# Linear attention into a SwiGLU block: reordering the first batches' attention, and group 0's layer 2, on one core

## The chip, the cores and the metric

The kernel runs on one core of a Trainium2 chip. A core has TensorE (PE, matrix multiplication, results into PSUM), VectorE (DVE), ScalarE (ACT), GpSimd (POOL) and SyncE (SP), each with its own queue of instructions, and 16 DMA engines. The metric is the device time of one execution in microseconds; lower is better.

## What is computed

```python
# q, k, v: 8 batches x 8 heads x 576 positions x 64;  phi(x) = elu(x) + 1
q_p, k_p = phi(q), phi(k)
kv  = einsum('bhsd,bhse->bhde', k_p, v)
z   = sum(k_p, axis=2)
num = einsum('bhsd,bhde->bhse', q_p, kv)
den = einsum('bhsd,bhd->bhs', q_p, z)[..., None] + 1e-06
x   = (num / den).transpose(0, 2, 1, 3).reshape(4608, 512)
g   = x @ w_gate                       # 512 x 1536
out = (g * sigmoid(g)) * (x @ w_val) @ w_out     # 1536 x 512
```

The kernel computes phi as max(x, 0) + min(exp(x), 1).

## The kernel before

Every batch of 576 positions is cut in 9 units of 64 (`J = 9`); 8 units make a group of 512 rows, so there are 9 groups for 8 batches (`NG = 9`), and group 1 holds the last unit of batch 0 and most of batch 1. For each group, layer 1 runs over 12 blocks of 128 hidden features (`fb`). Each block takes 8 matmuls of 128x512, four chunks of the 512 inputs for the gate and four for the value (`l1`, L285, or chunk by chunk with `l1_mm`, L270). ACT then takes silu of the gate half, and DVE multiplies it with the value half into `hT` (`l1_post`, L278). Layer 2 runs over four row tiles `t`, 12 matmuls each (`l2_mm`, L295), which `l2_out` (L311) moves from PSUM to `osb` and stores.

The attention of later batches is worked in between. For a batch, `exp_k`, `mx_k`, `mn_k` and `add_k` make phi(k) in `kp`; `kv_corner` (L176) makes k.v from it in 36 matmuls of 64x64 for each half of the heads (`lp`), with either `kp` alone, or the terms `kp` (holding the max) and `ek` (holding the min) one after the other; `r_copy` moves it to `R`. The sum over positions z is made in two ways. In batches 2 to 7, `zsum` on DVE and `zb` (L207) on PE and ACT spread it over the partitions; then `chain` (L506) makes den on DVE, for half of the heads at a time: `s3_prod`, `s3_reduce`, `s3_recip`, `s3_scale`, after which `dtr` (L229) transposes the scaled q by a DMA on SP's queue. In batches 0 and 1, which come before there is anything to hide behind, q is transposed on PE (`qtr`, L363), z is spread in `Zr`, den comes from PE by `t_corners(…, Zr, …)` (L411), `lnrd` (L399) makes 1/den on ACT as exp(-ln), and `x_t` (L407) multiplies num by it on DVE straight into the layer's input `xT`. `num` (L255) and `corners` (L247) make num in PSUM; `x_copy` (L261) copies it to `xT`.

PSUM is eight tiles of 128x512, used as four pairs; `ring` is the order in which `pair()` hands them out. `put_off` moves a pair to the end. The program text gives the order on every engine (the schedule is by hand), and waits between engines come from the tiles that are read and written.

At the start (L420 to L471) batch 0's attention is worked alone, then layer 1's first two blocks chunk by chunk. `warm(n)` (L120) issues `n` matmuls of 128x128 ones on PE whose result is not used; `WARM` (L43) holds how many at five places. Group 0's layer 2 is `layer2_0` (L527): all four tiles go along together, one `fb` at a time, and at given `fb` the steps `s0` to `s7` work on batch 1: transposes (`s0`, `s1`, `s3`), den (`s2`, `s4`), k.v (`s5`, `s6`), num (`s6`, `s7`), and in `s7` the last two units of batch 1 (`corners(…, 7, 9, …)`), which belong to group 2. The four evictions and the products of those last two units come at the end (`s8`). The main loop starts at L608; `block` (L516) works the attention of the next group ahead of tile 3. The line `gate` (L640) is a copy on GpSimd that reads the last transposed column, so that the loads after it in GpSimd's queue wait for it.

Of the kernel before, what the change touches and what calls it, by code (L numbers as in the profile page):

```python
# [13 lines left out]
P = 128  # L14
# [3 lines left out]
def kernel(  # L18
# [21 lines left out]
    EPS = 1e-6  # L40
    SC = 4096.0
    NB = 3
    WARM = (36, 10, 20, 8, 6)  # L43

    sb = ctx.enter_context(tc.tile_pool(name="sb", bufs=1))
    pp = ctx.enter_context(tc.tile_pool(name="ps", bufs=1, space=bass.MemoryType.PSUM))
# [50 lines left out]
    def put_off(p):  # L97
        pair(p)
# [18 lines left out]
    def act(out, in_, func=AF.Copy, scale=1.0, bias=0.0):  # L117
        nc.scalar.activation(out=out, in_=in_, func=func, bias=bias, scale=scale)  # L118

    def warm(n):  # L120
        for _ in range(n):
            nc.tensor.matmul(out=pp4[2][1][:, 0:P], lhsT=ones[:, :], rhs=ones[:, :], start=True, stop=True)

    def hs(lp):
        return slice(2 * lp, 2 * lp + 2)
# [13 lines left out]
    def mx_k(b, lp):  # L139
        nc.vector.tensor_scalar(out=jl(kp, b, lp), in0=lj(kr, b, lp), scalar1=0.0, scalar2=None, op0=ALU.max)  # L140
# [13 lines left out]
    def add_k(b, lp):  # L154
        a = kp[b % 2][:, lp, :, :]
        nc.vector.tensor_tensor(out=a, in0=ek[b % 2][:, lp, :, :], in1=a, op=ALU.add)  # L156
# [19 lines left out]
    def kv_corner(b, lp, t, first, last):  # L176
        ps = kvp[b]
        for j in range(J):
            for l2 in range(2):
                for hh in range(2):  # L180
                    rows = slice(C * hh, C * hh + C)
                    nc.tensor.matmul(out=ps[hh][D * l2:D * l2 + D, D * lp:D * lp + D],  # L182
                                     lhsT=t[b % 2][rows, lp, j, D * l2:D * l2 + D],
                                     rhs=vr[b % NB][rows, 2 * lp + l2, D * j:D * j + D],
                                     start=(first and j == 0), stop=(last and j == J - 1))
# [204 lines left out]
    def zt(b, lp, ps, t, first, last):  # L390
        for j in range(J):
            nc.tensor.matmul(out=ps[:, 0:2], lhsT=t[b % 2][:, lp, j, :], rhs=ob[:, 0:P:C],
                             start=(first and j == 0), stop=(last and j == J - 1))
# [17 lines left out]
    def t_corners(g, W, lp, ps):  # L411
        for (b, j0, j1, c0) in units(g)[1]:
            corners(ps, W[b], b, lp, j0, j1, c0)

    def t_add_half(lp, ps, h):
        a = qT[0][:, lp, 4 * h:4 * h + 4, :, :].rearrange("p j h c -> p (j h c)")
        nc.vector.scalar_tensor_tensor(out=a, in0=ps[:, 256 * h:256 * h + 256].bitcast(FP16), scalar=0.0, in1=a,
                                       op0=ALU.max, op1=ALU.add)
# [14 lines left out]
    ph[0][2]()  # L433
    mx_k(0, 0)
    zt(0, 0, pp4[3][0], kp, True, False)
    warm(WARM[3])
    mn_k(0, 0)
    zt(0, 0, pp4[3][0], ek, False, True)
    ph[1][1]()
    zr_copy(0, 0, pp4[3][0])  # L440
    warm(WARM[4])
    t_corners(0, Zr, 0, pp4[2])
    lnrd(pp4[2], 0)
    mx_k(0, 1)
    mn_k(0, 1)
    zt(0, 1, pp4[3][1], kp, True, False)
    zt(0, 1, pp4[3][1], ek, False, True)
    add_k(0, 0)
    kv_corner(0, 0, kp, True, True)
    zr_copy(0, 1, pp4[3][1])  # L450
    t_add_half(1, pq[1], 0)
    r_copy(0, 0, 1, "VV")
    t_add_half(1, pq[1], 1)
    t_corners(0, R, 0, pp4[0])
    x_t(0, 0, pp4[0], (0,))
    t_corners(0, Zr, 1, pp4[3])
    lnrd(pp4[3], 1)
    kv_corner(0, 1, kp, True, False)
    kv_corner(0, 1, ek, False, True)
    x_t(0, 0, pp4[0], (1,))  # L460
# [55 lines left out]
    def block(g):  # L516
        b1, b2 = g + 1, g + 2
        if b1 < NG:
            for lp in range(2):
                num(b1, lp)  # L520
                x_copy(b1, lp, "AV", 2 * C if b1 == 2 else 0)
        if b2 < B:
            kv_all(b2)
            r_copy(b2, 0, 2, "AA")
        put_off(l2p[(g, "p", 1)])

    def layer2_0():  # L527
        for t in range(4):
            l2_open(0, t)
        p1_z()  # L530
        p1_open()
        cq, dz = b1p["q"], b1p["z"]
        p8 = [t_phi_8(b, dz[0]) for b in range(2)]
        pm = [t_phi_main(1, lp, cq[lp]) for lp in range(2)]
        nc.scalar.preload_act_table_set("natural_log_exp_and_others")

        def den(lp, ps):
            t_corners(1, Zr, lp, ps)
            lnrd(ps, lp)

        def kvr(lp):
            kv_corner(1, lp, kp, True, True)
            r_copy(1, lp, lp + 1, "VV")

        def nx(lp, ps):
            t_corners(1, R, lp, ps)
            x_t(1, lp, ps)

        def s0():
            qtr(1, 0, cq[0])  # L550
            for f in pm[0]:
                f()

        def s1():
            qtr8(dz[0])
            for f in (0, 1, 2):
                for b in range(2):
                    p8[b][f]()

        def s2():  # L560
            den(0, dz)

        def s3():
            qtr(1, 1, cq[1])
            for f in pm[1]:
                f()

        def s4():
            den(1, cq)

        def s5():
            kvr(0)

        def s6():
            kvr(1)
            nx(0, cq)

        def s7():
            nx(1, dz)
            for lp in range(2):  # L580
                corners(cq, Zr[1], 1, lp, 7, 9, P * lp)
                corners(cq, R[1], 1, lp, 7, 9, 256 + P * lp)
            exp_k(2, 0)
            exp_k(2, 1)
            lnrd(cq, 0, 0, 256)

        def s8():
            for t in range(4):
                l2_out(0, t, "V")
            for l2 in range(2):  # L590
                xmul(xT[0][:, l2::2, 0:P], cq[l2][:, 256:512].rearrange("p (l c) -> p l c", l=2),
                     rd[0][:, l2, 0:256].rearrange("p (l c) -> p l c", l=2))

        step = {1: [s0], 3: [s1, s3], 6: [s2], 7: [s4], 9: [s5], 10: [s6], 11: [s7]}
        for fb in range(FB):
            if fb in step:
                for f in step[fb]:
                    f()
            for t in range(4):
                l2_mm(0, t, fb)  # L600
        s8()
        exp_q(2, 0)
        exp_q(2, 1)
        phi_k(2, 0)
        phi_k(2, 1)
        ring[:] = [dz, l2p[(0, "p", 0)], l2p[(0, "p", 1)], cq]

    for g in range(NG):  # L608
        b1, b2 = g + 1, g + 2
        if g == 0:  # L610
            sl = period0()
        else:
            sl, _ = none()
            if g == 1:
                sl[1] = [lam(zsum, b1)]
                sl[4] = [lam(phi_q, b1, 0), lam(zb, b1)]
                sl[5] = [lam(phi_q, b1, 1)]
                ch = chain(b1, 6)
            elif b1 < B:
                sl[0] = [lam(phi_q, b1, 0)]  # L620
                sl[1] = [lam(phi_q, b1, 1)]
                ch = chain(b1, 2)
            else:
                ch = {}
            for f, v_ in ch.items():
                sl[min(f, FB - 1)] += v_
        for fb in range(FB):
            if g == 0:
                if fb < 2:
                    continue  # L630
                if fb == 4:
                    ld2(k, kr, 2)
                    ld2(q, qr, 2)
                    ld2(v, vr, 2)
            l1(g, fb)
            for f in sl[fb]:
                f()
        if g + 3 < B:
            if g > 0:
                nc.gpsimd.tensor_copy(out=gate[:, :], in_=qT[b1 % 2][:, 1, J - 1, 1, C - 1:C])  # L640
            ld2(k, kr, g + 3)
            ld2(v, vr, g + 3)
            if g > 0:
                ld2(q, qr, g + 3)
        if g == 0:
            layer2_0()
            ld2(q, qr, 3)
        else:
            for t in range(4):
                if t == 0 and b2 < B:  # L650
                    exp_k(b2, 0)
                    exp_k(b2, 1)
                    exp_q(b2, 0)
                    exp_q(b2, 1)
                    phi_k(b2, 0)
                    phi_k(b2, 1)
                    zsum(b2)
                if g == 1 and t == 2:
                    kv_all(b1)
                    r_copy(b1, 0, 2, "AA")  # L660
                if t == 3:
                    block(g)
                if g == NG - 1 and t == 3:
                    l2_open(g, t)
                    o = None
                    for (n0, n1) in ((0, 256), (256, 512)):
                        for fb in range(FB):
                            l2_mm(g, t, fb, n0, n1)
                        o = l2_out(g, t, "V" if n0 == 0 else "A", n0, n1, o)
                    continue  # L670
                lay2(g, t)
                l2_out(g, t, "AV"[t % 2])
            if b2 < B:
                zb(b2)

# [29 lines left out]
```

## Time and profile before

| | us |
|---|---|
| median of 6 runs | 319.46 |
| the six runs | 319.17, 320.62, 319.76, 319.12, 320.64, 319.03 |
| the profiled execution | 319.38 |
| its span, first to last instruction | 317.5 |
| PE busy | 309.0 |
| DVE busy | 203.7 |
| ACT busy | 150.8 |
| POOL busy | 48.8 |

What lies around the span in the profiled execution is 319.38 - 317.5 = 1.9 us. In the views below, a line of the chain or the timeline begins with its start and its length in us, from the span's start. "x4" is four instructions merged in one line. The bracket at a line's end is the idle time of that engine before it and what ended it. PEld is the weight load, which overlaps matmuls.

### The profile page before, as it was taken

How to read it: one execution, taken by the hardware profiler on the slowest of the kernel's cores; microseconds unless marked ns; L12 is line 12 of the kernel's file. 1: busy time of each engine (PE TensorE's matmuls, PEld its weight loads, DVE VectorE, ACT ScalarE, POOL GpSimd, SP SyncE). 2: the span in 40 equal slices, each digit the busy share in tenths (PEclk: the TensorE clock that was granted, in tenths of full speed). 3: DMA queues.
4: the chain of work that ended last, by engine and by line, in shares of the span. 5: the costliest groups of instructions: out<-in, count | busy, mean ns of one | idle time of the engine just before them, and what ended most of it. 6: DMA issues, size and time to landing. Idle time of an engine off the chain costs nothing.

```text
span 317.5 us, 5702 instructions
## 1 busy us (share of the span) xinstructions
PE 309.0 (97%) x2276; PEld 146.9 (46%) x2276; DVE 203.7 (64%) x356; ACT 150.8 (47%) x227; POOL 48.8 (15%) x73
## 2 busy tenths in 40 slices
PE   7899999999999999999999999999999999999994
PEld 6634444444544454445444454445444444444443
DVE  3844866999759774987498749973992344234410
ACT  2865859737443574347534753375331333133311
POOL 8665333000500140005000600000000000000000
PEclk9989999999999999999999999999999999999999
DMA  8999999921793299038903790315023400140014
GB/s 157 195 198 199 206 206 206 254 46 37 124 234 59 56 125 233 2 74 124 236 1 74 113 241 6 61 28 121 0 42 67 99 3 1 33 101 0 0 33 101
DMA packets 41163, 32.52 MB, mean 102 GB/s; under 512 B 16432, under 2 KB 36400, under 8 KB 41136
## 3 DMA queue, kind: packets, MB, share of 16 engines
q0 software_dynamic: 20736, 18.58, 38.0%
q1 hardware_dynamic: 20320, 13.51, 17.5%
q8 instruction: 18, 0.29, 0.4%
q10 hardware_dynamic: 80, 0.07, 0.1%
q14 instruction: 9, 0.07, 0.1%
HBM read 37.75 MB, written 9.44 MB: 149 GB/s over the span
## 4 chain that ended last, share of the span: by engine, by line
PE 87%; ACT 5%; DVE 4%; DMA 2%; issue 1%; POOLq 0%
PE pp L289 54%; PE pp L296 27%; DMA qr<-in_q_dram 2%; PE pp L251 2%; PE pp L182 2%; PE pp L273 2%; DVE hT L282 1%; ACT lnt L118 1%; ACT ek L118 1%; ACT rd L118 1%; ACT eq L118 1%; PE pp L367 1%; ACT L118 0%; DVE den L217 0%; ACT sil L118 0%
## 5 line engine op out<-in xcount | busy, mean ns | idle before, releaser
L118 ACT ACTIVATE sil<-pp 128x512 f16<-128x512 f32 x108 | 63.3, 597 | 102.5 <-PE pp L289 96.1
L289 PE MATMUL pp<-xT,wg 128*128 128x512 f16 x424 | 108.8, 379 | 0.0
L289 PE MATMUL pp<-xT,wv 128*128 128x512 f16 x424 | 108.8, 379 | 0.0
L282 DVE SCALAR_TENSOR_TENSOR hT<-pp,sil 128x512 f16<-128x512 f32 x108 | 72.1, 681 | 47.8 <-PE pp L289 34.5
L296 PE MATMUL pp<-wo,hT 128*128 128x512 f16 (+1 forms) x444 | 97.7, 374 | 0.9 <-DVE osb L319 0.5
L296 PEld LDWEIGHTS <-hT 128*128 128x128 f16 x444 | 42.0, 98 | 49.4 <-issue 1.9
L289 PEld LDWEIGHTS <-wv 128*128 128x128 f16 x424 | 41.5, 98 | 50.1
L289 PEld LDWEIGHTS <-wg 128*128 128x128 f16 x424 | 41.5, 98 | 49.3
L319 DVE TENSOR_SCALAR osb<-pp 128x512 f32<-128x512 f32 (+1 forms) x20 | 13.2, 674 | 31.4 <-PE pp L296 31.4
L118 ACT ACTIVATE osb<-pp 128x512 f32<-128x512 f32 (+1 forms) x17 | 9.8, 578 | 34.9 <-PE pp L296 34.9
L118 ACT ACT_TABLE_LOAD x14 | 18.0, 1283 | 2.8 <-PE pp L289 2.6
L640 POOL COPY gate<-qT 128x1 f16<-128x1 f16 x4 | 1.6, 393 | 106.9 <-DVE hT L282 77.1
L118 ACT ACTIVATE ek<-kr 128x1152 f16<-128x1152 f16 x16 | 17.8, 1154 | 0.2
L226 DVE TENSOR_TENSOR qp<-qp,rden 128x1152 f16<-128x1152 f16 x12 | 16.2, 1346 | 0.0
L217 DVE TENSOR_REDUCE den<-prod 128x18 f32<-128x1152 f16 x12 | 16.1, 1345 | 0.0
L268 DVE TENSOR_SCALAR xT<-pp 128x512 f16<-128x512 f32 (+1 forms) x14 | 8.8, 667 | 7.4 <-PE pp L251 7.3
L118 ACT ACTIVATE eq<-qr 128x1152 f16<-128x1152 f16 x12 | 13.2, 1147 | 0.0
L101 POOL DMA_DIRECT2D vr<-in_v_dram x16 | 11.8, 741 | 5.2 <-DMA wo<-in_moe_w_out_dram 1.9
L101 POOL DMA_DIRECT2D kr<-in_k_dram x16 | 11.6, 725 | 5.9 <-DMA wo<-in_moe_w_out_dram 2.2
L101 POOL DMA_DIRECT2D qr<-in_q_dram x15 | 10.9, 730 | 5.7 <-DMA wo<-in_moe_w_out_dram 1.8
L156 DVE TENSOR_TENSOR kp<-ek,kp 128x1152 f16<-128x1152 f16 x15 | 11.4, 758 | 0.5
L144 DVE TENSOR_SCALAR ek<-ek 128x1152 f16<-128x1152 f16 x16 | 7.3, 457 | 6.1 <-ACT ek L118 6.1
(67 smaller groups left out, 179.0 us busy)
## 6 DMA issues: line engine op xcount, KB each, us to landing
out_dram<-osb SPq DMA_DIRECT2D x70, 128.0 KB, 4.8
kr<-in_k_dram POOLq DMA_DIRECT2D x16, 288.0 KB, 6.1
vr<-in_v_dram POOLq DMA_DIRECT2D x16, 288.0 KB, 9.0
qr<-in_q_dram POOLq DMA_DIRECT2D x15, 288.0 KB, 12.0
wo<-in_moe_w_out_dram POOLq DMA_DIRECT2D x3, 512.0 KB, 13.0
wg<-in_moe_w_gate_dram POOLq DMA_DIRECT2D x5, 256.0 KB, 9.2
wv<-in_moe_w_val_dram POOLq DMA_DIRECT2D x5, 256.0 KB, 9.7
q<-in_q_dram SPq DMA_DIRECT2D x1, 576.0 KB, 3.6
```

Of the source, the lines that this page charges most:

```text
L101: nc.gpsimd.dma_start(out=dst[b % NB][:, 2 * lp:2 * lp + 2, :], in_=src[b].rearrange("(l a) (c j) d -> (a c) l (j d)", a=2, j=J)[:, 2 * lp ...
L118: nc.scalar.activation(out=out, in_=in_, func=func, bias=bias, scale=scale)
L144: nc.vector.tensor_scalar(out=a, in0=a, scalar1=1.0, scalar2=None, op0=ALU.min)
L156: nc.vector.tensor_tensor(out=a, in0=ek[b % 2][:, lp, :, :], in1=a, op=ALU.add)
L182: nc.tensor.matmul(out=ps[hh][D * l2:D * l2 + D, D * lp:D * lp + D], lhsT=t[b % 2][rows, lp, j, D * l2:D * l2 + D], rhs=vr[b % NB][rows, 2 ...
L217: nc.vector.tensor_reduce(out=den[:, c, :], in_=prod[:, :, :].rearrange("p j (l d) -> p (j l) d", d=D), axis=AX.X, op=ALU.add)
L226: nc.vector.tensor_tensor(out=qv, in0=qv, in1=rden[:, c, :].unsqueeze(2).to_broadcast([P, 2 * J, D]), op=ALU.mult)
L268: nc.vector.tensor_scalar(out=dst, in0=ps[l2][:, c0:], scalar1=1.0 / SC, scalar2=None, op0=ALU.mult)
L282: nc.vector.scalar_tensor_tensor(out=hT[g % 2][:, fb, :], in0=ps[1][:, :], scalar=SC, in1=s[:, :], op0=ALU.mult, op1=ALU.mult)
L289: nc.tensor.matmul(out=ps[h][:, :], lhsT=w[:, c, P * fb:P * fb + P], rhs=xT[g % 2][:, c, :], start=(c == 0), stop=(c == 3))
L296: nc.tensor.matmul(out=l2p[(g, t)][:, n0:n1], lhsT=hT[g % 2][:, fb, P * t:P * t + P], rhs=wo[:, fb, n0:n1], start=(fb == 0), stop=(fb == F ...
L319: nc.vector.tensor_scalar(out=o[:, n0:n1], in0=ps[:, n0:n1], scalar1=1.0 / SC, scalar2=None, op0=ALU.mult)
```

## The change

It has three parts. In batch 0, the first half's k.v is made from the two terms instead of their sum, so `add_k` goes; the second half's work on `mx_k`, z and den moves ahead of the first num; q's second half is finished by one instruction over 1024 columns instead of two over 512; the dummy matmuls after the first three places are 256 columns wide and stand in other places and numbers. In group 0's layer 2, `fb` 0 to 7 run over all tiles as before, with the two den steps in one place, and then each tile's last four `fb` run together: tiles 0 and 1, k.v of batch 1, tile 2, num of the first heads, tile 3, num of the others. Tiles 0 to 2 are evicted as they end. The last two units of batch 1 move to `block(1)`. In group 1, layer 1's first two blocks take chunks 0 and 1 of both before chunks 2 and 3; `zb` comes one `fb` later; the second half of batch 2's den (reduce, reciprocal, scale, transpose) comes after layer 1; tile 1 is evicted by ACT; and the order of the PSUM ring is another.

```diff
@@ -40,7 +40,7 @@
     EPS = 1e-6
     SC = 4096.0
     NB = 3
-    WARM = (36, 10, 20, 8, 6)
+    WARM = (34, 14, 16, 7, 3, 5, 4)
 
     sb = ctx.enter_context(tc.tile_pool(name="sb", bufs=1))
     pp = ctx.enter_context(tc.tile_pool(name="ps", bufs=1, space=bass.MemoryType.PSUM))
@@ -117,9 +117,10 @@
     def act(out, in_, func=AF.Copy, scale=1.0, bias=0.0):
         nc.scalar.activation(out=out, in_=in_, func=func, bias=bias, scale=scale)
 
-    def warm(n):
+    def warm(n, w=1, ps=None):
         for _ in range(n):
-            nc.tensor.matmul(out=pp4[2][1][:, 0:P], lhsT=ones[:, :], rhs=ones[:, :], start=True, stop=True)
+            nc.tensor.matmul(out=(ps or pp4[2][1])[:, 256:256 + P * w], lhsT=ones[:, :],
+                             rhs=ones[:, :].unsqueeze(1).to_broadcast([P, w, P]), start=True, stop=True)
 
     def hs(lp):
         return slice(2 * lp, 2 * lp + 2)
@@ -433,28 +434,29 @@
     ph[0][2]()
     mx_k(0, 0)
     zt(0, 0, pp4[3][0], kp, True, False)
-    warm(WARM[3])
+    warm(WARM[3], 2)
+    ph[1][1]()
     mn_k(0, 0)
     zt(0, 0, pp4[3][0], ek, False, True)
-    ph[1][1]()
+    mx_k(0, 1)
     zr_copy(0, 0, pp4[3][0])
-    warm(WARM[4])
+    warm(WARM[4], 2)
     t_corners(0, Zr, 0, pp4[2])
     lnrd(pp4[2], 0)
-    mx_k(0, 1)
+    zt(0, 1, pp4[3][1], kp, True, False)
     mn_k(0, 1)
-    zt(0, 1, pp4[3][1], kp, True, False)
+    ph[1][2]()
+    kv_corner(0, 0, kp, True, False)
+    kv_corner(0, 0, ek, False, True)
     zt(0, 1, pp4[3][1], ek, False, True)
-    add_k(0, 0)
-    kv_corner(0, 0, kp, True, True)
+    r_copy(0, 0, 1, "VV")
     zr_copy(0, 1, pp4[3][1])
-    t_add_half(1, pq[1], 0)
-    r_copy(0, 0, 1, "VV")
-    t_add_half(1, pq[1], 1)
+    warm(WARM[5], 2, pp4[1][1])
+    t_corners(0, Zr, 1, pp4[3])
+    lnrd(pp4[3], 1)
     t_corners(0, R, 0, pp4[0])
     x_t(0, 0, pp4[0], (0,))
-    t_corners(0, Zr, 1, pp4[3])
-    lnrd(pp4[3], 1)
+    warm(WARM[6], 2, pp4[1][1])
     kv_corner(0, 1, kp, True, False)
     kv_corner(0, 1, ek, False, True)
     x_t(0, 0, pp4[0], (1,))
@@ -518,10 +520,21 @@
         if b1 < NG:
             for lp in range(2):
                 num(b1, lp)
+                if b1 == 2:
+                    corners(nump[(2, lp)], R[1], 1, lp, 7, 9, 0)
                 x_copy(b1, lp, "AV", 2 * C if b1 == 2 else 0)
         if b2 < B:
             kv_all(b2)
+            if b1 == 2:
+                for lp in range(2):
+                    corners(kvp[b2], Zr[1], 1, lp, 7, 9, 2 * P + P * lp)
             r_copy(b2, 0, 2, "AA")
+            if b1 == 2:
+                lnrd(kvp[b2], 0, 2 * P, 4 * P)
+                for lp in range(2):
+                    for l2 in range(2):
+                        w0 = 2 * P + P * lp
+                        xmul(xT[0][:, 2 * lp + l2, 0:P], nump[(2, lp)][l2][:, 0:P], rd[0][:, l2, w0:w0 + P])
         put_off(l2p[(g, "p", 1)])
 
     def layer2_0():
@@ -557,53 +570,41 @@
                 for b in range(2):
                     p8[b][f]()
 
-        def s2():
-            den(0, dz)
-
         def s3():
             qtr(1, 1, cq[1])
             for f in pm[1]:
                 f()
 
         def s4():
+            den(0, dz)
             den(1, cq)
 
-        def s5():
-            kvr(0)
-
-        def s6():
-            kvr(1)
-            nx(0, cq)
-
-        def s7():
-            nx(1, dz)
-            for lp in range(2):
-                corners(cq, Zr[1], 1, lp, 7, 9, P * lp)
-                corners(cq, R[1], 1, lp, 7, 9, 256 + P * lp)
-            exp_k(2, 0)
-            exp_k(2, 1)
-            lnrd(cq, 0, 0, 256)
-
-        def s8():
-            for t in range(4):
-                l2_out(0, t, "V")
-            for l2 in range(2):
-                xmul(xT[0][:, l2::2, 0:P], cq[l2][:, 256:512].rearrange("p (l c) -> p l c", l=2),
-                     rd[0][:, l2, 0:256].rearrange("p (l c) -> p l c", l=2))
-
-        step = {1: [s0], 3: [s1, s3], 6: [s2], 7: [s4], 9: [s5], 10: [s6], 11: [s7]}
-        for fb in range(FB):
-            if fb in step:
-                for f in step[fb]:
-                    f()
+        step = {1: [s0], 3: [s1, s3], 7: [s4]}
+        FO = 8
+        for fb in range(FO):
+            for f in step.get(fb, []):
+                f()
             for t in range(4):
                 l2_mm(0, t, fb)
-        s8()
+        for t in range(4):
+            if t == 2:
+                kvr(0)
+                kvr(1)
+            if t == 3:
+                nx(0, dz)
+            for fb in range(FO, FB):
+                l2_mm(0, t, fb)
+            if t < 3:
+                l2_out(0, t, "V")
+        nx(1, cq)
+        exp_k(2, 0)
+        exp_k(2, 1)
+        l2_out(0, 3, "V")
         exp_q(2, 0)
         exp_q(2, 1)
         phi_k(2, 0)
         phi_k(2, 1)
-        ring[:] = [dz, l2p[(0, "p", 0)], l2p[(0, "p", 1)], cq]
+        ring[:] = [l2p[(0, "p", 0)], dz, cq, l2p[(0, "p", 1)]]
 
     for g in range(NG):
         b1, b2 = g + 1, g + 2
@@ -611,11 +612,13 @@
             sl = period0()
         else:
             sl, _ = none()
+            late = []
             if g == 1:
                 sl[1] = [lam(zsum, b1)]
-                sl[4] = [lam(phi_q, b1, 0), lam(zb, b1)]
-                sl[5] = [lam(phi_q, b1, 1)]
+                sl[4] = [lam(phi_q, b1, 0)]
+                sl[5] = [lam(phi_q, b1, 1), lam(zb, b1)]
                 ch = chain(b1, 6)
+                late = ch.pop(10) + ch.pop(11)
             elif b1 < B:
                 sl[0] = [lam(phi_q, b1, 0)]
                 sl[1] = [lam(phi_q, b1, 1)]
@@ -632,7 +635,15 @@
                     ld2(k, kr, 2)
                     ld2(q, qr, 2)
                     ld2(v, vr, 2)
-            l1(g, fb)
+            if g == 1 and fb < 2:
+                if fb == 0:
+                    two = [pair(), pair()]
+                    for cs in ((0, 1), (2, 3)):
+                        for i in range(2):
+                            l1_mm(g, i, two[i], cs)
+                l1_post(g, fb, two[fb])
+            else:
+                l1(g, fb)
             for f in sl[fb]:
                 f()
         if g + 3 < B:
@@ -646,8 +657,12 @@
             layer2_0()
             ld2(q, qr, 3)
         else:
+            for f in late:
+                f()
             for t in range(4):
                 if t == 0 and b2 < B:
+                    if g == 1:
+                        nc.scalar.preload_act_table_set("natural_log_exp_and_others")
                     exp_k(b2, 0)
                     exp_k(b2, 1)
                     exp_q(b2, 0)
@@ -669,7 +684,7 @@
                         o = l2_out(g, t, "V" if n0 == 0 else "A", n0, n1, o)
                     continue
                 lay2(g, t)
-                l2_out(g, t, "AV"[t % 2])
+                l2_out(g, t, "A" if g == 1 and t == 1 else "AV"[t % 2])
             if b2 < B:
                 zb(b2)
 
```

## The prediction

> **What bounds the kernel now.** I read the page's busy shares and slices first, then the chain that ended last, then TensorE (PE) in order of time, then stages of granted clock.
>
> ```profile
> span 317.5 us, 5702 instructions
> ...
> PE 309.0 (97%) x2276; PEld 146.9 (46%) x2276; DVE 203.7 (64%) x356; ACT 150.8 (47%) x227; POOL 48.8 (15%) x73
> ...
> PE   7899999999999999999999999999999999999994
> ...
> PEclk9989999999999999999999999999999999999999
> ```
>
> PE bounds the program: 97% busy, two matmul lines hold 81% of the chain, and a 128x512 matmul starts every 0.2155 us (layer 1's 80 between 21.34 and 38.60 us give that). A change can win only where PE waits, runs slow, or does something else than those matmuls. That is the first 54 us and the third slice, where the clock digit is 8. The stages of clock, cut where it changes (columns: stage, its length, busy time and instructions of PE, weight loads, VectorE, ScalarE, GpSimd, then granted clock, DMA share, GB/s):
>
> ```profile
> 8.80:12.21 3.41, 2.79 (x54) 2.02 (x52) 2.35 (x7) 2.80 (x4) 1.53 (x3) 1.00 1.26 194
> 12.21:15.63 3.42, 2.50 (x113) 1.81 (x114) 3.42 (x9) 2.84 (x5) 2.76 (x4) 1.00 1.36 195
> 15.63:19.04 3.41, 3.41 (x51) 1.23 (x41) 1.10 (x4) 3.33 (x5) 2.35 (x5) 0.50 1.46 200
> ```
>
> For 3.41 us PE is granted half its clock, just as layer 1 starts, and the 3.42 us before are the emptiest of PE's (2.50 us busy) with VectorE (DVE) full. PE in order of time:
>
> ```profile
> 13.12 0.48 PE L182 MATMUL pp<-vr,kp 64*64 64x64 f16 x36 [0.27 <-DVE kp L156]
> 14.05 0.53 PE L251 MATMUL pp<-qT,R 64*64 64x512 f16 x2 [0.46 <-DVE R L198]
> ...
> 16.08 0.61 PE L273 MATMUL pp<-xT,wg 128*128 128x512 f16 x1
> 16.48 0.64 PE L273 MATMUL pp<-xT,wv 128*128 128x512 f16 x1
> ...
> 19.39 0.38 PE L273 MATMUL pp<-xT,wv 128*128 128x512 f16 x1
> ...
> 21.34 1.03 PE L289 MATMUL pp<-xT,wg 128*128 128x512 f16 x4
> ```
>
> Starts are 0.40 us apart at 16.1 us and 0.21 us apart at 19.4. The other two losses are in the chain, in group 1, where DVE is full from 54 to 84 us:
>
> ```profile
> 62.45 0.30 DVE zs L205
> 62.75 0.05 issue
> 62.79 0.28 PE pp L209
> ...
> 77.20 0.64 DVE hT L282
> 77.83 0.05 issue
> 77.88 2.98 PE pp L296 x13
> ```
>
> By starts, PE loses 62.79-62.37 = 0.42 us before the matmul of `zb`, and 77.88-(75.00+11x0.2155) = 0.51 us before tile 0's last layer-2 matmul, since `hT` 11 stands behind the den reduce on DVE.
>
> **What the Trainium skill says.** "TensorE: Matmul & The Clock Gate", Part 1 (What's actually happening): the clock is full or half, set from how busy PE was over free-running windows of about 3.4 us. The trace agrees: one stage at 0.50, 3.41 us long. The page says also that the window's phase varies from run to run; one profile can't show that, but the six times (319.03 to 319.17 three times, 320.62 and 320.64) would fit one more half-clock stage, worth up to 1.7 us. Same page, Back-to-back issue gap: a 256-column matmul costs 262 cycles, from which I estimate 0.11 us; the trace's 128-column dummies give 0.056 us (10 in 0.56), so twice that agrees. "ScalarE: Activation LUTs", What ACT_TABLE_LOAD costs: about 1283 ns; the profile's table loads take a mean of 1283.
>
> **The change part by part.** All sums are against the profiled execution (319.38 us, span 317.5), which is 0.08 us under the median of 319.46.
>
> *Batch 0's head, up to the first `l1`.* Until 10.9 us nothing that decides moves: transposes wait for `qr` to 7.6 us, exp to 10.4, `mn_k` to 10.88. The new ordering puts the second `mx_k` in DVE's gap at 10.9 and drops `add_k` (0.75): the first k.v runs from two terms, 36 more matmuls at 0.37 us per 36 (weight-load row). `mn_k` of the second half waits for its exp (9.23+2.46 = 11.69) and ends at 12.15; the whole `qT` multiply-add (1.22) ends at 13.3. PE: k.v 12.35 to 13.1, so it is done before DVE is free; the R copies end at 13.66 (before: 14.13), `zr_copy` at 13.9. Five wide dummies fill to 14.25, den of heads 1 runs to 14.68, num of heads 0 to 15.1 (0.41 to 0.43 per four 512-column matmuls). So `x_t` starts about 15.05, 0.35 later than the 14.69 of before, as num now stands behind den. Four more dummies (0.44) to 15.55; the second k.v (about 0.75 with its two terms) to 16.3. Its values are issued at 6.04 and land 8.7 us later, at 14.7, so moving ahead of that wins nothing. Layer 1's first matmul: 16.35 against 16.08.
>
> From there the clock decides. At full clock: four matmuls to 17.2, num of heads 1 (R ready at 16.9) to 17.65, DVE's two products at 18.3 and 18.95 (0.45 after num's start, 0.65 each), matmuls of the second chunk to 18.5, third to 19.4, fourth to 20.25. First L289: 20.25 instead of 21.34, **-1.1 us**. At half clock to 19.04 as before: first four to 18.06, num to 18.6, and the same sum gives 21.42, +0.1.
> Will it be full? Between 12.21 and 15.63 the change adds nine wide dummies (0.98 us) and 36 matmuls (0.37) on PE and pulls num and den together, where before 0.9 us were empty. Between 8.80 and 12.21, where the clock stayed full, old and new dummies are equal (1.4 us of columns). What threshold holds, no trace shows: bounds 0 and -1.1; I take -1.1.
>
> *Group 0's layer 2.* Before: 38.60 to 53.74 = 15.14 us, of which 48x0.2155 = 10.34 are layer 2. The rest by starts: z 0.06, transposes 0.66 and 0.90, den 0.45 and 0.46, k.v 0.51, k.v with num 0.74, num with the tail's corners 1.00. After: 0.06+0.66+0.90, the two den together 0.80 (one change of shape fewer, 0.1), both k.v 0.85 (the 72 of group 1: 80.68 to 81.53), num 0.45 twice: 4.17, **-0.62**. Of it 0.46 are the 16 corner matmuls of batch 1's last units, which go to group 1. New waits in it: kvr's R copies have tile 2 (0.86) as cover and need 0.72; num 1 needs rd of heads 1, eight ScalarE steps of 0.63 from 8.2 us after layer 1's end, so at 13.2, and is asked for at 14.0; if this cover went, 0.2 us. The first two `fb` of group 1 take chunks 0 and 1 of both pairs first: 8x0.2155 = 1.7 us as cover for the two last products (1.3). Before no PE wait stood there either: 0.
>
> *Group 1.* Three of four evictions (0.62 each) now run beside layer 2 and ScalarE loses the tail's 1.7 us, so DVE is some 2 us ahead. `zb` one slot later: **-0.42**. The second den half (reduce, reciprocal, scale, transpose) stands behind `hT` 11: **-0.51**. Its scale still ends 4.1 us after layer 1 (79.08-75.0), the same sum of work; its transpose lands 3.3 us later (row of `qT`), +7.4, and num of heads 1 asks at +9.1, cover 1.7. On SP only this transpose is behind it, then output stores, tile 0's eviction being later anyway. Corners: **+0.46** (0.115 per four). The tail's Ln/Exp (1.7 us) come on ScalarE after the last R copies, 46.3 to 48.0 counted from group 0's layer-1 end; then four products of 0.23 to 0.28 on DVE; group 2's first matmul waits for the third, at 48.6, while PE comes at 48.65. Bounds 0 and +0.5; I take +0.1. The table is loaded by hand once in place of the automatic one: 0. The gate copy on GpSimd now stands ahead of the moved transpose in program order, so batch 4's six loads (1.4 us apart, as the six before them are) go out some 30 us sooner, behind batch 3's; they may slow the first transpose, which has some 9 us to spare: 0.
>
> Groups 2 to 8 keep their work. Sum: -1.1-0.62-0.42-0.51+0.46+0.1 = -2.1, from 319.38: 317.3; rounding for small waits, **317.4 us**. Layer 2 comes 1.1 us earlier, but `qr` of batch 1 (issued at 27.22, landed 13.0 us later) is asked for at 40.9, so that doesn't bind.
>
> **Rivals.**
> - *The half clock stays where it was.* For: the trace gives no threshold, and 36 of the added matmuls are 64x64. Against: 1.3 us more PE work in the window. -1.0+0.1: 318.5.
> - *Group 1 gives its gain back*: the tail's products and num hold PE for 0.5 us each instead of 0.42 and 0.51. Then -1.1-0.62+0.46+0.3 or so: 318.4. For: ScalarE order is tight to 0.1 us; against: DVE is 2 us ahead.
> - *Slower: two half-clock stages.* If the stage 8.80 to 12.21 counts as idle (dummies 36 and 20 shrink to 34 and 16 at its head), PE is at half from 12.21 as well. Nine wide dummies (+1.0) and eight 512-column matmuls (+0.85) lie on the path to layer 1, most of it uncovered: +1.7, and the second stage +0.1; with -1.0 from the rest, 320.2. It decides from the point where that earlier stage drops; before, with 2.79 us busy, it held.
>
> **How the numbers follow.** Forecast 0.57, half clock stays 0.19, gain given back 0.09, two stages 0.15. The likeliest's own range is 316.6 to 318.0 (tail 0 to 0.5, changes of shape 0.3 either way). To leave out no more than 0.2, up to 319.2, which holds the two middle cases; low 316.5. Faster by over 0.3% (0.96 us, about what a measurement here can tell from none) means under 318.5: all of the first, most of the third, half of the second, 0.74. Same 0.14, slower 0.12.
>
> **What would show it.** Right: no stage at 0.50 after 12 us, first L289 near 20.3; group 0's layer 2 in 14.5 us; no PE wait before `zb` or tile 0's last matmul; group 1 from its first layer-1 start to group 2's in 34.2 us (before 34.66). Wrong: a half-clock stage anywhere from 12 us on, or a wait at group 2's first matmul for DVE.

## The result and the profile after

The median is 317.3 us over 30 executions (316.71 to 319.58), against 319.56 us over 65 of the kernel before. The ratio is 0.9938, 95% interval 0.9927 to 0.995, so 1.6 to 2.3 us faster; the forecast was 317.4. The profiled execution took 317.38 us with a span of 315.6, 1.9 us less than before's.

From the profile's page, busy shares and granted clock in tenths:

```profile
PE 308.3 (98%) x2315; PEld 147.6 (47%) x2315; DVE 204.5 (65%) x355; ACT 151.3 (48%) x228; POOL 48.4 (15%) x73
...
PEclk9999999999999999999999999999999999999999
```

The 8 in the clock row is gone. The two stages of 3.41 us up to layer 1's start, counted on from 6.27 us, where this trace's record of the clock begins (5.39 us in the profile before), and PE where layer 1 starts:

```profile
9.68:13.10 3.42, 3.26 (x119) 2.54 (x120) 3.09 (x7) 2.76 (x4) 1.90 (x3) 1.00 1.30 200
13.10:16.51 3.41, 3.12 (x100) 1.88 (x98) 2.19 (x8) 3.25 (x6) 2.70 (x4) 1.00 1.39 196
```

```profile
16.07 0.39 PE L274 MATMUL pp<-xT,wg 128*128 128x512 f16 x1
16.29 0.38 PE L274 MATMUL pp<-xT,wv 128*128 128x512 f16 x1
...
20.02 1.03 PE L290 MATMUL pp<-xT,wg 128*128 128x512 f16 x4
```

Layer 1's first matmul starts where it did (16.07, before 16.08), but the starts are 0.22 us apart, not 0.40, and its first full block starts at 20.02 instead of 21.34: 1.32 us. The next lines are from the chain that ended last, in group 0's layer 2 and group 1, and below them PE in order of time, from tile 1 to tile 2 of that layer 2:

```profile
28.04 13.06 DMA qr<-in_q_dram
...
41.15 0.25 PE pp L376 x2
...
48.70 0.45 DVE osb L320
...
49.30 0.23 DVE R L199
...
63.27 0.11 PE pp L210
63.38 10.36 PE pp L290 x48
73.74 5.18 PE pp L297 x24
```

```profile
45.90 2.76 PE L297 MATMUL pp<-wo,hT 128*128 128x512 f16 x12
...
49.57 0.61 PE L183 MATMUL pp<-vr,kp 64*64 64x64 f16 x36 [0.50 <-DVE R L199]
50.11 1.04 PE L297 MATMUL pp<-wo,hT 128*128 128x512 f16 x4
```

Two waits in group 0's layer 2 are new: PE waits for `q` of batch 1 (to 41.10), and before the second k.v for an eviction and the `R` copies behind it on DVE (to 49.57). The two waits of before are gone: around `zb` and before layer 2 of group 1 the chain runs on PE alone. PE's lines where the stages of the program begin, first before, then after:

```profile
38.60 0.19 PE L492 MATMUL pp<-ob,zs 128*128 128x2 f16 x2
...
53.74 1.03 PE L289 MATMUL pp<-xT,wg 128*128 128x512 f16 x4
...
88.40 1.03 PE L289 MATMUL pp<-xT,wg 128*128 128x512 f16 x4
```

```profile
37.28 0.19 PE L494 MATMUL pp<-ob,zs 128*128 128x2 f16 x2
...
52.74 0.39 PE L274 MATMUL pp<-xT,wg 128*128 128x512 f16 x1
...
86.49 1.04 PE L290 MATMUL pp<-xT,wg 128*128 128x512 f16 x4
```

By these starts:

| stage | before | after |
|---|---|---|
| to the end of group 0's layer 1 | 38.60 | 37.28 |
| group 0's layer 2, to group 1's first layer-1 matmul | 15.14 | 15.46 |
| group 1, to group 2's first | 34.66 | 33.75 |
| sum | 88.40 | 86.49 |

So in these two profiles 1.32 us came from the head, 0.91 from group 1, and layer 2 gave 0.32 back.

### The profile page after: what moved, and what is told of

Its sections match the earlier page's. It is cut to its first block, busy times and chain, and to the rows that moved or that the text cites. A ratio compares the mean times of both kernels' runs of the same rounds, so it can differ in the third digit from the quotient of the medians.

```text
span 315.6 us, 5774 instructions
## 1 busy us (share of the span) xinstructions
PE 308.3 (98%) x2315; PEld 147.6 (47%) x2315; DVE 204.5 (65%) x355; ACT 151.3 (48%) x228; POOL 48.4 (15%) x73
## 4 chain that ended last, share of the span: by engine, by line
PE 85%; DMA 11%; POOL 2%; issue 1%; DVE 0%; ACT 0%; POOLq 0%; DVEq 0%
PE pp L290 51%; PE pp L297 29%; DMA qr<-in_q_dram 4%; DMA kr<-in_k_dram 3%; DMA vr<-in_v_dram 3%; PE pp L252 2%; PE pp L183 1%; PE pp L274 1%; POOL wg L110 0%; POOL wv L110 0%; POOL kr L101 0%; DVE osb L320 0%; POOL qr L101 0%; POOL vr L101 0%; PE pp L210 0%
## 5 line engine op out<-in xcount | busy, mean ns | idle before, releaser
L290 PE MATMUL pp<-xT,wg 128*128 128x512 f16 x416 | 106.8, 379 | 0.0
L290 PE MATMUL pp<-xT,wv 128*128 128x512 f16 x416 | 106.8, 379 | 0.0
L290 PEld LDWEIGHTS <-wv 128*128 128x128 f16 x416 | 40.7, 98 | 49.1
L290 PEld LDWEIGHTS <-wg 128*128 128x128 f16 x416 | 40.6, 98 | 48.6 <-DVE xT L406 0.3
L157 DVE TENSOR_TENSOR kp<-ek,kp 128x1152 f16<-128x1152 f16 x14 | 10.6, 759 | 0.5
```

The source lines that it names most:

```text
L290: nc.tensor.matmul(out=ps[h][:, :], lhsT=w[:, c, P * fb:P * fb + P], rhs=xT[g % 2][:, c, :], start=(c == 0), stop=(c == 3))
```

## Experiments

**The head alone, and the rest alone.** The first takes the new head (WARM, `warm` and the code from `pq = pp4[0]` to the ring's setting) into the kernel before; the second takes the old head into the changed kernel.

```diff
# head alone: the kernel before, with
-    WARM = (36, 10, 20, 8, 6)
+    WARM = (34, 14, 16, 7, 3, 5, 4)
...
# rest alone: the changed kernel, with
-    WARM = (34, 14, 16, 7, 3, 5, 4)
+    WARM = (36, 10, 20, 8, 6)
...
```

> The kernel before with the new head of batch 0 alone (order and wide dummies), layer 2 and group 1 as before. My theory: the head brings most of the gain by keeping PE's clock full, so no stage at 0.50 from 12 us on, the first full layer-1 block starts 1.1 to 1.4 us sooner than the 21.34 us of before, ratio to before about 0.996 (318.2 us). Rival (the gain is that of group 1 alone): ratio 0.999 to 1.0.

> The changed kernel with the head of batch 0 as it was before: group 0's layer 2 and group 1 new. My theory: the half-clock stage at layer 1's start is there again; layer 2 costs 15.2 to 15.5 us (before 15.14), group 1 takes 33.8 us (before 34.66), so 0.6 us gained, ratio 0.998 (318.9 us). If the head brings nothing, this one is as fast as the changed kernel, 0.994.

Measured: head alone 318.07 us, ratio 0.9947 (0.9928 to 0.9965); rest alone 318.63 us, 0.9964 (0.9949 to 0.9979). Both bring a part. In the profile of the head alone the first full block of layer 1 starts at 20.23 us, 1.11 sooner than before; in that of the rest alone layer 2 takes 15.22 us and group 1 33.76, as expected. But that execution had its clock full with the *old* head, which I had not expected:

```profile
11.77:15.19 3.42, 2.50 (x127) 1.73 (x126) 3.42 (x9) 2.85 (x5) 2.63 (x4) 1.00 1.36 196
15.19:18.60 3.41, 3.41 (x43) 1.41 (x31) 1.84 (x5) 3.29 (x5) 2.52 (x4) 1.00 1.46 199
```

PE is as busy in the first stage, 2.50 us, as it was in the kernel before, where the next stage was granted 0.50; here it is granted 1.00. One profile therefore doesn't say how often a kernel has the half-clock stage. The mean granted clock of every execution tells more: one stage of 3.41 us at half is 3.41x0.5/317 = 0.54%, so a mean of about 0.995, and two give 0.989. A stage at half that begins after PE's last matmul lowers the mean too, but costs PE nothing; the profile before has one, and its mean is 0.992 with one stage at layer 1. So single executions may be sorted wrongly. The table sorts them at 0.9965 and 0.9915; for the kernel before it takes those that were run beside the experiments (one of its 43, at 0.982, would have three stages).

| kernel | executions | no half-clock stage: number, median | one | two or more |
|---|---|---|---|---|
| before | 94 | 3, 318.21 us | 48, 319.12 | 43, 320.15 |
| changed | 30 | 24, 317.14 us | 6, 319.25 | 0 |
| head alone | 8 | 8, 318.07 us | 0 | 0 |
| rest alone | 22 | 4, 316.84 us | 9, 318.42 | 9, 319.22 |

Without a stage the old head is no slower: 318.21 against 318.07 us, and within the new rest 316.84 against 317.14. As far as so few executions of the old head can tell (3 and 4), what the head brings is that stages become rare, and nothing else.

**Dummies alone, none, and narrow ones.** Three kernels separate the dummies from the new order. In the first the kernel before gets nine wide dummies in PE's empty places and nothing else; in the second the changed kernel loses all dummies after the third place; in the third it keeps them all at 128 columns.

```diff
# dummies alone: the kernel before, with the new warm(), and
     add_k(0, 0)
+    warm(3, 2, pp4[3][0])
     kv_corner(0, 0, kp, True, True)
+    warm(4, 2, pp4[3][0])
...
     t_corners(0, R, 0, pp4[0])
+    warm(2, 2, pp4[3][0])
# none: the changed kernel, with
-    WARM = (34, 14, 16, 7, 3, 5, 4)
+    WARM = (34, 14, 16, 0, 0, 0, 0)
# narrow: the changed kernel, with
-            nc.tensor.matmul(out=(ps or pp4[2][1])[:, 256:256 + P * w], lhsT=ones[:, :],
-                             rhs=ones[:, :].unsqueeze(1).to_broadcast([P, w, P]), start=True, stop=True)
+            nc.tensor.matmul(out=(ps or pp4[2][1])[:, 256:256 + P], lhsT=ones[:, :],
+                             rhs=ones[:, :], start=True, stop=True)
```

> The kernel before with nothing changed but nine wide dummies put in PE's empty places between the first k.v and the second (3 ahead of the first k.v, 4 after it, 2 after the first num), at most 0.1 us on the path. Clock theory: no stage at 0.50, up to 1.4 us gained, ratio 0.996. Rival (the order gains): ratio 1.0, since nothing that decides moves.

> The changed kernel without any dummy matmul after the first three places (7, 3, 5 and 4 wide ones gone, 2.1 us of PE work between 9.8 and 15.4 us). Clock theory: half-clock stages are back in most executions, about 1.5 to 2.2 us each, so 318.5 to 319.5 us. Rival (the order with its 36 more matmuls keeps the clock by itself): 317.0, as with the narrow ones.

> The changed kernel with the same number of dummies in the same places, all of 128 columns, so that they are half as long where they were wide. Clock theory: a stage at 0.50 comes back near layer 1's start, the time goes up by 1.2 to 2.2 us against the changed kernel, ratio to before 0.998 to 1.0. Rival (the order of the head is what gains): clock or not, the first layer-1 matmuls are where they are in the changed kernel, ratio 0.994.

Measured: dummies alone 318.26 us, 0.9964 (0.9948 to 0.9981), 12 of 14 executions without a stage. None: 318.67 us, 0.9975 (0.9963 to 0.9986), and not one of 22 without a stage, 16 with two. Narrow: 317.24 us, 0.9925 (0.9899 to 0.9952), 5 of 6 without a stage. So nine dummies in the old order do what the whole new head does, to 0.2 us, and the new order without dummies doesn't do it. The expectation for narrow ones failed: half their length is enough in most executions.

That leaves a rival open. All dummies of the narrow kernel together are 83 matmuls of 128 columns, and the kernel before has 80 of them, 14 of them in two places where the kernel without dummies has none. So with hardly more dummy work than before the new head kept the clock. It has the dummies in other places and the attention in another order; which of the two did it there isn't separated. The stages of the kernel without dummies:

```profile
9.57:12.98 3.41, 1.83 (x79) 1.41 (x82) 2.70 (x7) 2.80 (x3) 2.16 (x3) 1.00 1.30 202
12.98:16.39 3.41, 3.03 (x138) 2.18 (x124) 2.10 (x6) 3.31 (x7) 2.52 (x5) 0.50 1.41 194
16.39:19.81 3.42, 3.42 (x14) 0.95 (x12) 1.48 (x5) 2.37 (x3) 2.35 (x4) 0.50 1.45 197
```

After 1.83 us of PE work in 3.41 the clock fell. But it stayed at half after a stage in which PE was busy 3.03 us, most of it with matmuls whose weights are 64x64, and 2.50 us went both ways above. PE's busy time in the profile alone is not what decides it. The stages also begin at another time in each profile (one begins at 8.80 us before, at 9.68 after, at 9.57 here, at 8.36 with the rest alone), so that other work falls into one. What decides is open.

**Group 1: each move undone, then both.** The second den half goes back into layer 1; `zb` goes back one block; then both.

```diff
# den:
-                late = ch.pop(10) + ch.pop(11)
+                late = []
# zb:
-                sl[4] = [lam(phi_q, b1, 0)]
-                sl[5] = [lam(phi_q, b1, 1), lam(zb, b1)]
+                sl[4] = [lam(phi_q, b1, 0), lam(zb, b1)]
+                sl[5] = [lam(phi_q, b1, 1)]
```

> The changed kernel with the second half of batch 2's den chain back in layer 1 of group 1. My theory: PE waits again for hT 11, 0.5 us at tile 0's last matmul; group 1 from its first layer-1 matmul to group 2's takes 34.2 instead of 33.75 us. Rival (DVE is 2 us ahead now, so the wait is gone anyway): 33.75 us.

> The changed kernel with zb of batch 2 back one block earlier. My theory as in the prediction: PE waits 0.4 us for zsum, group 1 takes 34.15 us. Rival (DVE is ahead now, zsum is done in time): 33.75 us.

> The changed kernel with both moves in group 1 undone: zb one block earlier and the second den half in layer 1. Each alone cost nothing. Theory: DVE is ahead since the evictions run beside layer 2 and the tail has left the start of group 1, so both undone cost nothing either, group 1 takes 33.7 us. Rival: each covers for the other, and together 0.4 to 0.9 us come back (34.2 to 34.6).

Measured by stage: group 1 takes 33.68 us with den back, 33.74 with `zb` back, 33.82 with both (changed kernel 33.75); medians 317.61, 317.29 and 317.01 us. The rivals of the first two hold, and the theory of the third: neither move gains anything here, alone or with the other. PE in the kernel with both undone shows no wait before `zb` or inside tile 0:

```profile
63.54 0.27 PE L210 MATMUL pp<-zs,ob 128*128 128x256 f16 x1
75.73 5.38 PE L297 MATMUL pp<-wo,hT 128*128 128x512 f16 x24
```

**Evictions at the end again.** From the kernel with both moves undone, the evictions of group 0 go back to the end of its layer 2, with layer 1's first two blocks one after the other and the old ring, which goes with that order.

```diff
-            if t < 3:
-                l2_out(0, t, "V")
         nx(1, cq)
         exp_k(2, 0)
         exp_k(2, 1)
-        l2_out(0, 3, "V")
+        for t in range(4):
+            l2_out(0, t, "V")
...
-        ring[:] = [l2p[(0, "p", 0)], dz, cq, l2p[(0, "p", 1)]]
+        ring[:] = [dz, l2p[(0, "p", 0)], l2p[(0, "p", 1)], cq]
...
-            if g == 1 and fb < 2:
+            if g == 99 and fb < 2:
```

The last line makes the interleaved branch one that no group takes.

> The one with both moves undone, and besides with the four evictions of group 0 at the end of its layer 2, layer 1's first two blocks of group 1 one after the other and the ring as before. The tail stays in group 1's block. If the evictions' place is what puts DVE ahead, PE waits for zsum and for hT 11 again (0.3 and 0.3 us in the list of PE's waits), and group 1 takes 34.3 us or more. If it is the tail that went, no wait, 33.8 us.

Group 1 takes 35.41 us (33.82 with the evictions early), the median is 319.27 us, ratio 0.9993 (0.9974 to 1.0011). Of the executions without a half-clock stage the medians are 319.05 us (10) against 317.01 (11). The waits before `zb` and in tile 0 are back, and two at layer 1's start besides, as PE's list of waits has it (us in total, times, longest; the lines with L183 are k.v of batch 0 and of batch 1, on which more is said below):

```profile
PE pp L183 <- DMA vr<-in_v_dram: 1.0, 1, 1.0
...
PE pp L290 <- DVE xT L406: 0.5, 2, 0.3
...
PE pp L183 <- DVE R L199: 0.4, 1, 0.4
PE pp L297 <- DVE hT L283: 0.3, 1, 0.3
...
PE pp L210 <- DVE zs L206: 0.2, 1, 0.2
```

DVE's first instruction on batch 2's k, before, after, and in this kernel:

```profile
56.69 0.45 DVE L140 TENSOR_SCALAR kp<-kr 128x1152 f16<-128x1152 f16 x1
```

```profile
54.78 0.45 DVE L141 TENSOR_SCALAR kp<-kr 128x1152 f16<-128x1152 f16 x1
```

```profile
58.60 0.45 DVE L141 TENSOR_SCALAR kp<-kr 128x1152 f16<-128x1152 f16 x1
```

Counted from group 1's first matmul (53.74, 52.74, 54.83) that is 2.95, 2.04 and 3.77 us; with both undone it is 2.04 again. The 1.73 us from 2.04 to 3.77 are near three evictions of 0.62. So DVE's lead comes from the evictions leaving its queue in group 1, and with it go the waits before `zb` and in tile 0. That the tail moved away isn't enough. Three things go back in this kernel together: by starts the two waits at layer 1's start take 0.86 of the 1.59 us, and which share of these is the interleaved start's is not separated.

**k.v split, and q loaded first.** Layer 2's two new waits are taken away: the first k.v goes ahead of tile 1, so that tile 1 covers the R copies; in the second kernel the second half of `q` is loaded ahead of `wo`'s rows 4 to 7 too.

```diff
-            if t == 2:
+            if t == 1:
                 kvr(0)
+            if t == 2:
                 kvr(1)
# second kernel also:
-    ld_w2(4, 8)
     ld(q, qr, 1, 1)
+    ld_w2(4, 8)
```

> The changed kernel with batch 1's k.v of the first heads ahead of tile 1 and that of the second heads ahead of tile 2, instead of both ahead of tile 2. The second then doesn't wait for the R copies of the first. My theory: the 0.50 us wait of PE for R goes, one change of shape (0.1) is added; group 0's layer 2 takes 15.0 us instead of 15.46; ratio to the changed kernel 0.9987. Rival (another wait takes its place, ScalarE's Ln reading the same PSUM pair): 15.3 to 15.5 us.

> The changed kernel with k.v of batch 1 split around tile 1, and with the second half of batch 1's q loaded ahead of layer 2's weight rows 4 to 7. My theory: the 0.50 us wait for R and the wait of up to 0.4 us for q (seen in some executions) are gone; group 0's layer 2 takes 14.6 us in every execution; ratio to before 0.991 to 0.992 (316.7 us). Rival: the weight rows now come late and PE waits for them instead, 15 us.

Layer 2 takes 14.59 us with the split, less than the 15.0 expected, and 14.60 with both. Medians are 316.92 and 316.66 us; ratios 0.9933 (0.9906 to 0.9959) and 0.9908 (0.9886 to 0.993). The wait for `q` isn't in the profile of the first either (it is 0.4 us in that of den back, absent with `zb` back), so what loading `q` first is worth isn't shown. PE of the second kernel, with k.v in two pieces and no wait before the second:

```profile
47.96 0.50 PE L183 MATMUL pp<-vr,kp 64*64 64x64 f16 x36
48.39 1.04 PE L297 MATMUL pp<-wo,hT 128*128 128x512 f16 x4
49.36 0.48 PE L183 MATMUL pp<-vr,kp 64*64 64x64 f16 x36
```

**Both, with narrow dummies.** The second kernel above, with the narrow `warm` of the earlier diff.

> The same as the one with k.v split and q first, but with all dummies 128 columns wide. If the wide ones lie 0.4 us on the path and narrow ones keep the clock as well, 316.3 us; if they keep it less often, the median stays at 316.7 or above and single executions at 318.5 come more often.

Median 316.21 us, ratio 0.9908 (0.9879 to 0.9938). Four executions without a stage have a median of 316.13 us (the wide ones 316.66 in six), two with one stage 317.31 and 318.13. Both kernels are faster than the one before, and both medians lie below the changed kernel's 317.3, though the intervals of the ratios still touch its own (0.9927 to 0.995). Which of them is better, six executions each don't settle, since it hangs on how often a stage comes.

## Why the prediction was right, and where it was not

- *The head, -1.1 us.* Measured 1.32 in the profiles, by the mechanism named: full clock at layer 1's start. The other 0.2 is the first matmul, forecast at 16.35 us and found at 16.07, where it was (16.28 with the head alone). Sorted by clock, the medians say the same: the kernel before loses 319.56-318.21 = 1.35 us to stages at its median (318.21 is of three executions), and the changed kernel's median execution has none. What the prediction only supposed, that some executions of the kernel before have two stages, holds for 43 of 94. That nine dummies are enough in the old order, and that the new order fails without any after the third place, is shown; what the new order adds isn't. The threshold stayed as open as the prediction left it.
- *The rival with the half clock still there, 318.5 us.* Six of 30 executions are that case, but their median is 319.25. One stage costs the changed kernel 2.1 us, where the prediction had 1.2, and it cost the kernel before 0.9. The traces point to a term that the prediction has at nothing: `v`'s first half. The change moved the first k.v from 13.12 to 12.24 us. Two profiles with all of the new head have the half-clock stage, that with both moves undone and that with the evictions at the end, and in both PE waited 1.0 us for `v` ahead of this k.v (the first line of the list above). There `v` landed 9.5 to 9.9 us after its loads were issued, against 8.1 and 9.1 in the changed kernel's profile. The wait doesn't decide the clock alone: the kernel with k.v split and `q` first has it too, and its clock stayed full. That the changed kernel's six executions are of this kind fits the price, as a stage costs 2.6 us with both moves undone and 2.0 with the evictions at the end, but none of the six was profiled.
- *Group 0's layer 2, -0.62.* Wrong: +0.32. The term that was mis-sized is "both k.v 0.85": from tile 1's end (45.90+12x0.2155 = 48.49) to tile 2's start at 50.11 it took 1.62. I gave num the R copies as its wait, but the second k.v itself waits for them. That tile 1's eviction stands ahead of them on DVE is the smaller part: with the evictions at the end the wait is still 0.40 us, not 0.50. Split around tile 1, the stage takes 14.6 us, the 14.52 of the sum. Another 0.29 is `q`: I had it land at 40.2, with layer 2 asking at 40.9; it landed at 41.1. In profiles where it came in time (`zb` back, both undone) layer 2 takes 15.17 us, as long as before. The two den together took 0.68 and not 0.80.
- *Group 1: `zb` -0.42 and den -0.51.* Both waits went, but not for the reason given: they stay away with both moves undone. DVE being ahead, which the prediction named before them, does it alone (by 0.9 us and not 2, since the products of num, which DVE works first, now start 0.95 us before group 1's first matmul instead of 2.56). I charged the same gain to two edits that had nothing left to remove. The stage as a whole gained 0.91, where 0.47 was forecast (0.93 less the corners' 0.46), and part of this is luck: the corners cost less (the eight matmuls with Zr take 0.23, and the num with the eight others in it takes 0.46 as a whole, 0.42 without them), and the k.v after num went from 1.05 to 0.65 us, which the prediction has nowhere; what made it slow before isn't shown.
- *Tail, +0.1.* It fits: the third product ends as PE arrives, and from `zb` to group 2's first matmul PE takes 0.17 us, 0.11 with the head alone.
- *The slower rival, two stages.* None of 30 executions had two; without dummies 16 of 22 did, at a median of 318.85 us.
- *The price of a matmul.* The 80 matmuls give 17.26/80 = 0.2158 us and not 0.2155, which moves a sum over 48 of them by 0.01.

The forecast of 317.4 was thus right in total with layer 2 0.9 us too good, group 1 0.5 too poor and the head 0.2 too poor. Only the head's gain came in size and by the mechanism forecast; that the other two errors nearly cancel is luck.

## What to carry to other kernels

When PE's waits before a dense stage are filled with matmuls that nobody reads, count how many executions keep the full clock, not what one profile shows; here nine of them in the gaps were worth as much as the whole new head. When an engine is saturated over a stage, first take work off it that could run earlier, and only then move single waits: the moves may have nothing left to gain. Of a step that is merged, check what the second half of the merged step waits for. And of a step that is moved forward, check when its loads land, in a slow execution too.

## What the runs showed of the hardware

The granted clock is not a property of the kernel alone: 94 executions of one program, sorted by their mean clock, gave no half-clock stage 3 times, one 48 times and two or more 43 times, with medians of 318.21, 319.12 and 320.15 us. And PE's busy time in a stage of 3.4 us didn't decide the next one: 2.50 us was followed by half in one kernel and by full in another, 2.35 us by full in a third (k.v split and `q` first, 11.99 to 15.40 us), and 3.03 us at half, most of it with 64x64 weights, by another half. The loads also move between executions: `q`'s second half, with the same queue ahead of it, let PE start its transposes at 7.06 to 7.85 us in the profiles of kernels whose loads up to there are the same, and `v`'s halves landed between 7.6 and 9.9 us after their issue.
